# Layer 0's first MLP pair with seven block products for w4, and block sums of the weights added in DRAM

## The chip, the cores and the metric

The kernel runs on one core of a Trainium2 chip. The metric is device time in microseconds, lower is better. TensorE (PE) multiplies, VectorE (DVE) and ScalarE (ACT) do elementwise work, GpSimd (POOL) does small pieces of it, SyncE (SP) issues the DMAs. PEld is TensorE's loading of weights.

## The reference

Two layers, each an FNet mixing step and a shift MLP, on `x` of 2048 rows by 512 columns in float32:

```python
x = x + real(DFT_seq(DFT_hidden(layernorm(x))))         # dense DFT matrices
u = layernorm(x)
h = gelu(layernorm(u) @ w1)                             # 512 x 512
x1 = u + shift_quarters(h, +1, -1, +2, -2) @ w2         # 512 x 512
x = x + x1 + gelu(layernorm(x1) @ w3) @ w4              # 512 x 1376, 1376 x 512
```

## The kernel before

**Arithmetic.** Every float32 operand is kept as a rounded high part and a low part, the difference. A product is three matmuls (`mm3`, lines 294 to 296): high by high, high by low, low by high. ACT casts the high part, DVE subtracts for the low part. The weights of the matmuls lie 128 by 128 on the array; 512 or 256 columns stream past them.

**Fewer products.** Several matrix products are done by blocks with seven products in place of eight, after Strassen and Winograd: sums of blocks are made on both sides, and products are added up. On the weights' side of w3 a pair of 128-column tiles is cut in four blocks, and seven units per pair of tiles are kept: four block sums (units 0 to 3), three blocks as they are (4 to 6). The same holds for w4 in layer 1. In layer 0, w3 goes by seven products, w4 by eight.

**Order.** All work is in an order written out by hand (`manual_schedule`): each engine takes its instructions in the order of the program, so a step put at some place of the loop stands, on its engine, behind all that was put before it. One layer runs as follows.

- Layer 0's chunk 0 has a plain phase (`plain_phase`), in which the DFT's sequence product is made block by block. It calls `hook(0)` to `hook(15)`, one before each 24 matmuls.
- Each chunk c of 512 rows has an x phase (`x_phase`, for c > 0 in layer 0) and a y phase (`y_phase`). In the x phase eight steps k each call `hook(2k)` before 12 matmuls (banks C and B) and `hook(2k+1)` before 6 (bank A, with the DFT block's difference, an item "one"); ahead of `hook(2k)` stand 0, 12 or 24 matmuls of the hidden DFT of the chunk before (`HAT`). The y phase calls `hook(k)` before the first half of a step.
- DFT blocks come by DMA into four raw buffers (`raw`, line 222), are cast by ACT (lines 240, 243, 247) and completed by DVE (line 257) in a ring of four slots. `stream()` hands out the next slot and prepares the one three further.
- `by_pairs` then does the MLPs. First the spatial-shift part: 32 slots of 12 matmuls (`shifted`, `mixed`), with steps for DVE and ACT attached to slot numbers (`D(slot, ...)`, `A(slot, ...)`). Then two pairs of chunks go through w3, gelu and w4.

**The pairs.** In layer 0 both pairs run the loop over five pairs of tiles in `by_pairs`: seven w3 products (`prod`, 6 matmuls each), gelu, and w4 on the tiles before (`w4_part`, 12 matmuls of 512 columns for a tile and a chunk). In layer 1 the first pair is `first_pair`: w3 by seven products for all five pairs of tiles, the gelus kept, then 39 steps (`multiply`, 12 matmuls of 256 columns each) that take w4 by seven products; the second is `last_pair`.

**Weights.** The raw weights lie in `w34`. `w4_split(i)`, called from the plain phase's hooks i and from chunk 1's x phase as `w4_split(16 + i)`, takes 12 blocks of 128 by 512 (one of w3, 11 of w4) through four SBUF places `w4in`, one step per hook: block n is loaded by SP at hook n + 3, cast by ACT at n + 4, completed by DVE and stored by SP at n + 5 (to `w4d`, `w3e`). At one hook the store of block n − 2 comes first, then the cast of n − 1, then the load of n:

```python
for n in (i - 5, i - 4, i - 3):
    if n == i - 5:    # DVE low part; SP: dma_start(w4_from[n][1], w)
    elif n == i - 4:  # ACT: copy(w[:, 0], wf[:, 1])
    else:             # SP: dma_start(wf[:, 1], w4_from[n][0])
```

`w4_sums(k, i)` makes w4's block sums of one pair of tiles in SBUF, in five x phases of both layers (`W4_AT`), for layer 1's use. The units of w3 are made in layer 0's shift part (first pair of tiles) and in its first pair's loop (`w_prep`): SP loads `staged`, DVE makes four sums, ACT and DVE split them, SP keeps the result in `w3d`. Layer 0's second pair and layer 1 load `w3d`.

**Queues.** All DMAs are issued by SP, in the program's order; POOL issues none, and has only the small power and product steps of the layer norms (lines 313, 314, 334, 335).

Of the kernel before, what the change touches and what calls it, by code (L numbers as in the profile page):

```python
# [8 lines left out]
F32 = mybir.dt.float32  # L9
# [4 lines left out]
P = 128  # L14
# [29 lines left out]
def spectral_mlp_kernel(ctx: ExitStack, tc: tile.TileContext, x, ws, hs, w1, w2, w34, out):  # L44
# [7 lines left out]
    ident = const.tile([P, P], F32, name="ident")  # L52
    make_identity(nc, ident)
# [9 lines left out]
    w4s = [dram.tile([P, 4, 2, 2 * P], F32, name=f"w4s{i}") for i in range(NF // 2)]  # L63
    xtd = [dram.tile([D, CH], F32, name=f"xtd{i}") for i in range(2)]
# [52 lines left out]
    staged = at("staged", STG, 2, 2, 2 * P, dtype=F32)  # L117
# [19 lines left out]

    for i in range(WARM):
        nc.tensor.matmul(PD[1][:, :P], ident, ident, start=True, stop=True)  # L139
# [486 lines left out]
    def gelu(g, ps):  # L626
        order = "p (q b j) -> p b q j", "p (b q j) -> p b q j"
        g_of, ps_of = (v.rearrange(o, b=NB, q=TC) for v, o in zip((g, ps), order))
        nc.scalar.activation(g_of, ps_of, AF.Gelu_apprx_tanh)
# [79 lines left out]
    def b_sum(o, a, b):  # L709

        add(*(blkf[i][:, :, 1] for i in (o, a, b)), ALU.subtract)
# [12 lines left out]
    def by_pairs(layer, zs, xin, dst):  # L724
# [71 lines left out]
        order = [None] + fs + fs  # L796
        n_pairs = NC // 2
        seq, used = {"n": 0}, {"n": 0}

        def w4_slot(n):  # L800

            return n % 6 if n < len(order) else (n - len(order)) % 4

        def w4_load():
            n = seq["n"]
            if n == n_pairs * len(order) or n >= len(order) and n - used["n"] > 3:
                return
            src, i = order[n % len(order)], w4_slot(n)
            nc.sync.dma_start(w4r[i].bitcast(F32), w3e if src is None else w4d[src])
            seq["n"] += 1  # L810
# [4 lines left out]
        def w4_use():  # L815
            used["n"] += 1
            return w4r[w4_slot(used["n"] - 1)]

        def w3_load(n):
            if n >= n_pairs * (NF // 2):  # L820
                return
            if layer or n >= NF // 2:
                i = (n + (last_of(layer) and n >= NF // 2)) % 2
                nc.sync.dma_start(w3b[i].bitcast(F32), w3d[n % (NF // 2)])
                return
            nc.sync.dma_start(staged.rearrange("p f k w -> p f (k w)"), w34[2 * n : 2 * n + 2, :, 0].rearrange("f p w -> p f w"))

        def w3_sums(n, half):

            lo, (a, b) = w3bf[n % 2][:, 1], (staged[:, i] for i in range(2))  # L830
            if half == 0:
                add(lo[:, 2], a[:, 0], b[:, 0], ALU.subtract)
                add(lo[:, 0], b[:, 0], b[:, 1])
            else:
                add(lo[:, 1], lo[:, 0], a[:, 0], ALU.subtract)
                add(lo[:, 3], a[:, 1], lo[:, 1], ALU.subtract)

        def w3_of(n):
            return (slice(0, 4), w3bf[n % 2][:, 1, 0:4]), (slice(4, 6), staged[:, 0]), (slice(6, 7), staged[:, 1, 1:2])

        def w3_highs(n, *which):
            for i in which:
                units, src = w3_of(n)[i]
                nc.scalar.copy(w3b[n % 2][:, 0, units], src)

        def w3_lows(n, *which):
            w = w3b[n % 2]
            for i in which:
                units, src = w3_of(n)[i]
                nc.vector.tensor_tensor(w[:, 1, units], src, w[:, 0, units].bitcast(F32), op=ALU.subtract)  # L850

        def w3_keep(n):
            nc.sync.dma_start(w3d[n], w3b[n % 2].bitcast(F32))
# [63 lines left out]
        D(26, sum_of("t1", "12", "t1"))  # L917
# [10 lines left out]
        A(28, *([w3e_load] if last_of(layer) else [w4_load] * 4))  # L928
        if layer == 0:
            A(19, lambda: w3_load(0))  # L930
            D(23, lambda: w3_sums(0, 0))
            A(23, lambda: w3_highs(0, 1, 2))
            D(24, lambda: w3_sums(0, 1))
            A(24, lambda: w3_highs(0, 0))
            D(25, lambda: w3_lows(0, 0, 1, 2))
            A(25, lambda: w3_load(1))
            A(28, lambda: w3_keep(0))
        else:
            A(26, lambda: w3_load(0))
            A(28, lambda: w3_load(1))  # L940
            D(27, u_stats(2, 2))
            D(30, add_u(2, 0, 1, 2, 3))
# [16 lines left out]
        if not last_of(layer):  # L959
            w4_load()  # L960
            w4_load()
        gs = [tmp[:, 4], tmp[:, 5]]

        def w4_part(acc, f, h, beside=None):
            s = w4_use()
            for q in range(TC):
                if q == 2 and beside:
                    beside()
                v = slice(q * P, (q + 1) * P)
                mm3(acc[q], h[:, 0, v], h[:, 1, v], s[:, 0], s[:, 1], f == fs[0], f == fs[-1])  # L970
# [5 lines left out]
        bg, prep = [], {}  # L976

        def at_point(i):
            for f in prep.pop(i, ()):
                f()  # L980
# [60 lines left out]
        def z3_steps0(turned):  # L1041
            t = tmp[:, 0:4]
            return [
                lows("t3", "t4"),
                u_stats(2, 2),
                add_u(2, 0, 1, 2, 3),
                u_stats(3, 0),
                norm3(2, 0, 1),
                norm3(2, 2, 3),
                u_stats(3, 2),  # L1050
                lambda: (turn3(turned, 2, 0, 1)(), add_u(3, 0, 1)()),
                lambda: (turn3(turned, 2, 2, 3)(), turn_out(turned, z3d[2]), norm3(3, 0, 1)()),
                add_u(3, 2, 3),
                lambda: (norm3(3, 2, 3)(), turn3(t, 3, 0, 1)()),
                lambda: (turn3(t, 3, 2, 3)(), turn_out(t, z3d[3])),
            ]

        def next_block(c, half, to):
# [3 lines left out]
            4: [sum_of("t1", "12", "11")],  # L1062
# [9 lines left out]
        for pair in range(n_pairs):  # L1072
            c1, c2 = 2 * pair, 2 * pair + 1
            if last_of(layer):
                if pair == n_pairs - 1:
                    last_pair(c1, c2, dst, lambda: w4r[0])
                    continue
                loads = [next_block(*b) for b in ((3, 0, "12"), (2, 0, "11"), (2, 1, "21"), (3, 1, "22"))]
                first_pair(c1, c2, dst, z3_steps, loads, next_parts, w3_load, w3e_load)
                continue  # L1080
            kept, next_too = bool(layer or pair), pair == n_pairs - 1 and not last_of(layer)
            hcs = [hc[:, f] for f in range(NF)]
            if next_too:
                hcs[8:] = [hx[:, 0], hx[:, 1], rest[0]]
                bg += early
            if pair:
                bg.insert(0, lows("t4"))
            sets = [rest[4:8], rest[4:8]]
            bk, acc1 = (acc4, mm4) if pair == 0 else (mm4, acc4)
            acc2 = [bk[(1 + i) % 4] for i in range(4)]  # L1090
            if pair == 0:
                bg += z3_steps0(hc[:, 6:10])
            tmps[:] = gs
            s = w4_use()
            for i, names in enumerate((("11", "21"), ("12", "22"))):
                for d in range(KD):
                    b = blk[names[d // 2]]
                    v = slice(d * P, (d + 1) * P)
                    mm3(bk[i], s[:, 0, v], s[:, 1, v], b[:, d % 2, 0], b[:, d % 2, 1], d == 0, d == KD - 1)
                if i == 0:  # L1100
                    gelu_split(h4[2], bk[0], act)
                else:
                    gelu(hcs[NF - 1], bk[1])
                one()
            w4_load()

            def split_later(k):
                if k < NF:
                    split(h4[(2 + k) % 4], hcs[fs[k]], act)

            def next_blocks(*which):

                for c, half, to in which:
                    b_in(c, half, to)

            def w_prep(p):

                n = p + 1
                if n == NF // 2:
                    return {}  # L1120
                return {
                    0: [lambda: w3_sums(n, 0), lambda: w3_highs(n, 1, 2)],
                    1: [lambda: w3_sums(n, 1), lambda: w3_highs(n, 0)],
                    2: [lambda: w3_lows(n, 1, 2), *[lambda: w3_load(n + 1)] * (n + 1 < NF // 2)],
                    4: [lambda: w3_lows(n, 0), lambda: w3_keep(n)],
                }

            for p in range(NF // 2):
                prep = {} if kept else w_prep(p)
                u, v, x, y = sets[p % 2]  # L1130
                w = w3b[(5 * pair + p) % 2]
# [7 lines left out]
                if pair:  # L1139
                    one()  # L1140
# [791 lines left out]
```

## Time and profile before

| | |
|---|---|
| median of 3 runs | 1420.42 us (1420.28 to 1420.55) |
| profiled execution | 1420.21 us |
| its span, first to last instruction | 1418.3 us |
| TensorE clock granted | 1.0 throughout |
| bytes moved | 306.31 MB, 216 GB/s |

The profile is one execution. Its page gives each engine's busy time, the span in 40 slices with busy tenths, the DMA queues, the chain of work that ended last, and the costliest groups. Answers to narrower questions give a stretch's busy times, or single instructions with start and duration in us and, in brackets, how long their engine was idle before and what released it. "ACT w4in L1662: 10.5, 9" under "who waited for it" reads: these instructions' tiles kept line 1662 on ACT waiting 10.5 us in all, at 9 places. A queue named SPq is SP's issue of DMAs; "to landing" is from issue to the data being there.

### The profile page before, as it was taken

To read this page: it belongs to the slowest core of one execution; us is meant where nothing else is said; L and a number is where in the kernel's file an instruction comes from. 1 tells how busy PE (TensorE), PEld (TensorE's weight loads), DVE (VectorE), ACT (ScalarE), POOL (GpSimd) and SP (SyncE) were. 2 spreads that over 40 slices of the span, in tenths; PEclk is the share of its full clock that TensorE was granted. 3 is DMA by queue.
4 is the path that set the end of the run, shared out by engine and by line. 5 is a ranking of instruction groups with operands and counts; after the bars stand their busy time and mean duration, and the time that the engine had idled before them with its cause. 6 is when DMAs were issued, how large, how long until landed. Compare 5 with 4: busy or idle time off the path is not lost.

```text
span 1418.3 us, 17864 instructions
## 1 busy us (share of the span) xinstructions
PE 1413.0 (100%) x6465; PEld 1177.7 (83%) x6465; DVE 1186.4 (84%) x1675; ACT 740.8 (52%) x1007; POOL 77.9 (5%) x105
## 2 busy tenths in 40 slices
PE   9999999999999999999999999999999999999998
PEld 8888888888888888888888888888888888899887
DVE  7986998988979888666789989989889788897676
ACT  6663464455566754434555544644555656454351
POOL 2100000000001000000000000000000020000000
PEclk9999999999999999999999999999999999999999
DMA  7867647658753857945556476575597457677864
GB/s 256 278 208 237 208 153 262 194 164 308 240 164 98 292 205 261 357 159 187 193 176 214 149 262 200 172 262 169 194 309 238 134 141 245 189 247 240 311 207 158
DMA packets 136488, 306.31 MB, mean 216 GB/s; under 512 B 9680, under 2 KB 58064, under 8 KB 133712
## 3 DMA queue, kind: packets, MB, share of 16 engines
q1 hardware_dynamic: 136400, 305.17, 64.6%
q8 instruction: 51, 0.84, 0.2%
q14 instruction: 37, 0.30, 0.1%
HBM read 250.87 MB, written 54.26 MB: 215 GB/s over the span
## 4 chain that ended last, share of the span: by engine, by line
PE 94%; DVE 3%; ACT 1%; issue 1%; POOL 0%; DVEq 0%; POOLq 0%; ACTq 0%
PE psd L294 10%; PE psd L295 10%; PE psd L296 9%; PE psa L295 8%; PE psa L294 8%; PE psa L296 8%; PE psc L295 7%; PE psb L295 7%; PE psb L294 7%; PE psb L296 7%; PE psc L296 7%; PE psc L294 7%; DVE rest L480 0%; ACT tmp L342 0%; PE psd L139 0%
## 5 line engine op out<-in xcount | busy, mean ns | idle before, releaser
L240 ACT CAST ring<-raw 128x1024 fp32r<-128x1024 f32 x127 | 133.1, 1052 | 79.3 <-PE psd L296 43.2
L257 DVE TENSOR_TENSOR ring<-raw,ring 128x1024 fp32r<-128x1024 f32 x126 | 153.4, 1219 | 13.1 <-ACT ring L240 12.9
L294 PE MATMUL psd<-ring,rr 128*128 128x512 f32 x208 | 80.9, 389 | 0.0
L295 PE MATMUL psd<-ring,rr 128*128 128x512 f32 x208 | 80.9, 389 | 0.0
L296 PE MATMUL psd<-ring,rr 128*128 128x512 f32 x208 | 80.9, 389 | 0.0
L334 POOL TENSOR_TENSOR rs<-ve,mhalf 128x4 f32<-128x4 f32 x16 | 27.0, 1685 | 723.9 <-DVE nm L333 723.9
L247 ACT CAST ring<-ring0f 128x1024 fp32r<-128x1024 f32 x28 | 29.5, 1054 | 50.7 <-DVE ring0f L246 50.7
L257 DVE TENSOR_TENSOR ring<-ring1f,ring 128x512 fp32r<-128x512 f32 (+1 forms) x56 | 53.2, 950 | 0.7 <-ACT ring L243 0.7
L313 POOL TENSOR_TENSOR rs<-ve,mhalf 128x2 f32<-128x2 f32 (+2 forms) x33 | 28.8, 873 | 415.1 <-DVE nb L312 405.6
L342 ACT ACTIVATE tmp<-xs,nb,rs 128x512 f32<-128x512 f32 x56 | 43.3, 810 | 15.6 <-POOL nb L314 14.4
L294 PE MATMUL psc<-ring,ay 128*128 128x512 f32 x128 | 49.8, 389 | 0.0
L295 PE MATMUL psc<-ring,ay 128*128 128x512 f32 x128 | 49.8, 389 | 0.0
L296 PE MATMUL psc<-ring,ay 128*128 128x512 f32 x128 | 49.8, 389 | 0.0
L294 PE MATMUL psb<-ring,ay 128*128 128x512 f32 x128 | 49.8, 389 | 0.0
L295 PE MATMUL psb<-ring,ay 128*128 128x512 f32 x128 | 49.8, 389 | 0.0
L296 PE MATMUL psb<-ring,ay 128*128 128x512 f32 x128 | 49.8, 389 | 0.0
L295 PE MATMUL psa<-ring,ay 128*128 128x512 f32 x126 | 49.0, 389 | 0.0
L296 PE MATMUL psa<-ring,ay 128*128 128x512 f32 x126 | 49.0, 389 | 0.0
L294 PE MATMUL psa<-ring,ay 128*128 128x512 f32 x126 | 49.0, 389 | 0.0
L294 PE MATMUL psd<-ring,ay 128*128 128x512 f32 x126 | 49.0, 389 | 0.0
L295 PE MATMUL psd<-ring,ay 128*128 128x512 f32 x126 | 49.0, 389 | 0.0
L296 PE MATMUL psd<-ring,ay 128*128 128x512 f32 x126 | 49.0, 389 | 0.0
(826 smaller groups left out, 4488.7 us busy)
## 6 DMA issues: line engine op xcount, KB each, us to landing
raw<-in_ws SPq DMA_DIRECT2D x183, 512.0 KB, 5.1
raw<-in_hs SPq DMA_DIRECT2D x56, 512.0 KB, 3.6
w4r<-w4d SPq DMA_DIRECT2D x44, 512.0 KB, 4.6
w3b<-w3d SPq DMA_DIRECT2D x10, 1792.0 KB, 9.0
w3d<-w3b SPq DMA_DIRECT2D x5, 1792.0 KB, 6.8
x1d<-tmp SPq DMA_DIRECT2D x12, 512.0 KB, 6.2
xs<-x1d SPq DMA_DIRECT2D x12, 512.0 KB, 5.0
w4d<-w4in SPq DMA_DIRECT2D x11, 512.0 KB, 4.8
```

The source lines that it names most:

```text
L240: nc.scalar.copy(dest[:, a:b, 0], r[0][:, a:b])
L247: nc.scalar.copy(dest[:, :, 0], lo)
L257: nc.vector.tensor_tensor(lo, src, hi.bitcast(F32), op=ALU.subtract)
L294: nc.tensor.matmul(o, lh, rh, start=first, stop=False, skip_group_check=more)
L295: nc.tensor.matmul(o, lh, rl, start=False, stop=False, skip_group_check=more)
L296: nc.tensor.matmul(o, ll, rh, start=False, stop=last, skip_group_check=more)
L313: nc.gpsimd.tensor_tensor(rs[:, :n], ve[:, :n], mhalf[:, 0, :n], op=ALU.pow)
L334: nc.gpsimd.tensor_tensor(rs, ve, mhalf[:, :, :2], op=ALU.pow)
L342: nc.scalar.activation(o, s, AF.Identity, bias=mr[2], scale=mr[1])
```

## The change

- Layer 0's first pair now runs `first_pair`, as layer 1's does; the loop in `by_pairs` is left with layer 0's second pair, and w4 tiles come through four SBUF places, not six.
- All units of w3 and w4 are made ahead of the pair. `w4_split` becomes `w_split` with 20 entries: behind the 12 of before stand five of w3's blocks 4 and 5 and three loads with the blocks 6 of two pairs of tiles (the last has one). The appended ones run on into chunk 1's x phase.
- The block sums are made in DRAM tensors `sum3` and `sum4`. Step 0 of `sums_of` is five copies by SP (one per pair of tiles) of one block into four places; steps 1 to 3 are five DMAs each, issued by POOL, that add a block onto places 0 to 2, 1 to 3 and 2. w3's steps stand at hooks 0, 4, 8 and 12 of chunk 1's x phase, w4's at those of chunk 2's.
- The sums are loaded, split and kept at hooks of chunks 1 to 3 (`sum_at`) and, for two sums of w4, in the shift part.
- Signs change so that all weight sums are additions; units are in another order; some sums of activations and gelus take the sign. `first_pair` runs one of the last steps earlier. Chunk 2's statistics and residual sums move into the shift part in layer 0, too.
- The identity for the first matmuls lies in the arena. POOL's DMA scratch is 1024 bytes for 512.

```diff
-    w4_from = [(w34[NF - 1][:, 0], w3e)] + [(w34[f + LAG][:, 1], w4d[f]) for f in range(NF)]
-    def w4_split(i):
...
-    def w4_sums(k, i):
...
+    halves3 = [w34[2 * i : 2 * i + 2, :, 0].rearrange("f p (h w) -> f h p w", h=2) for i in range(NF // 2)]
+    halves4 = [w34[2 * i + LAG : 2 * i + LAG + 2, :, 1].rearrange("f p (h w) -> h f p w", h=2) for i in range(NF // 2)]
+    split_from = [(w34[NF - 1][:, 0], [w3e])] + [(w34[f + LAG][:, 1], [w4d[f]]) for f in range(NF)]
+    split_from += [(w34[2 * i][:, 0], [w3d[i][:, :, 4:6].rearrange("p r u w -> p r (u w)")]) for i in range(NF // 2)]
+    for i in range(0, NF // 2, 2):
+        src = w34[2 * i + 1 : min(2 * i + 5, NF - 1) : 2, :, 0, 2 * P :].rearrange("f p w -> p f w")
+        split_from.append((src, [w3d[k][:, :, 6] for k in range(i, min(i + 2, NF // 2))]))
+    def w_split(i):
+        for n in (i - 5, i - 4, i - 3):
...
+    def sums_of(to, blocks, i):
+        (r, c), (a, b) = (((1, 0), (0, 4)), ((0, 0), (0, 3)), ((1, 1), (1, 4)), ((0, 1), (2, 3)))[i]
+        for k in range(NF // 2):
+            src = blocks[k][r, c].unsqueeze(1).broadcast_to([P, b - a, 2 * P])
+            if i:
+                nc.gpsimd.dma_start(to[k][:, a:b], src, accum_op=ALU.add)
+            else:
+                nc.sync.dma_start(to[k][:, a:b], src)
...
+    for i in range(4):
+        prepare[1, "x", 4 * i] = [lambda i=i: sums_of(sum3, halves3, i)]
+        prepare[2, "x", 4 * i] = [lambda i=i: sums_of(sum4, halves4, i)]
+    sum_at(1, "y", sum_a, 3, 0, 3, 5, 6)
+    sum_at(2, "x", sum_a, 3, 1, 0, 4, 5)
+    sum_at(2, "x", sum_b, 3, 3, 1, 5, 6)
+    sum_at(2, "x", sum_a, 3, 2, 7, 11, 12)
+    sum_at(2, "y", sum_a, 3, 4, 1, 3, 4)
+    sum_at(3, "x", sum_a, 4, 0, 1, 5, 6)
+    sum_at(3, "x", sum_b, 4, 2, 2, 6, 7)
+    sum_at(3, "x", sum_a, 4, 1, 8, 12, 13)
...
@@ x phase, layer 0: hook(i)
-                    w4_split(2 * NP + i)
+                    w_split(2 * NP + i)
-                if (layer, c) in W4_AT:
-                    w4_sums(W4_AT[layer, c], i)
+                if layer == 0:
+                    prepare_at(c, "x", i)
...
@@ by_pairs
+        first_pair(0, 1, dst, z3_steps, loads, next_parts, w3_load, w3e_load if last_of(layer) else w4_load)
-        nc = bacc.Bacc("TRN2", target_bir_lowering=False, num_devices=1, dynamic_dma_scratch_size=512)
+        nc = bacc.Bacc("TRN2", target_bir_lowering=False, num_devices=1, dynamic_dma_scratch_size=1024)
```

The four numbers behind `sum_at`'s places and kind are the pair of tiles and the hooks of the load, the cast and the low part with the stores.

More of the change, by code (lines that the diff above doesn't have):

```diff
@@ L816, in w4_use @@
             used["n"] += 1
-            return w4r[w4_slot(used["n"] - 1)]
+            return w4r[(used["n"] - 1) % 4]
         def w3_load(n):
[L820 to L853, printed above, removed]
+            if n < n_pairs * (NF // 2):
+                nc.sync.dma_start(w3b[(n + (n >= NF // 2)) % 2].bitcast(F32), w3d[n % (NF // 2)])
         sc0, sc1, sc2 = scratch
@@ L1417, in first_pair @@
                 drain(n - 2)
-        for n, c in ((-2, c1), (-1, c2)):
-            drain(len(steps) + n)
-            for j in range(c * TC, c * TC + TC, 2):
-                rows(xs[j // 2], dst, j, 2, False)
+        drain(len(steps) - 1)
+        for j in (*range(c2 * TC, c2 * TC + TC, 2), *range(c1 * TC, c1 * TC + TC, 2)):
+            rows(xs[j // 2], dst, j, 2, False)
         w3_load(nk + 1)
```

482 lines of the change are left out of this document (215 added, 267 removed).

## The prediction

> **What bounds the kernel now.** I read the page's first, second and fourth parts, then stretches of the run one by one.
>
> ```profile
> span 1418.3 us, 17864 instructions
> PE 1413.0 (100%) x6465; PEld 1177.7 (83%) x6465; DVE 1186.4 (84%) x1675; ACT 740.8 (52%) x1007; POOL 77.9 (5%) x105
> DMA  7867647658753857945556476575597457677864
> PE 94%; DVE 3%; ACT 1%; issue 1%; POOL 0%; DVEq 0%; POOLq 0%; ACTq 0%
> ```
>
> TensorE is busy from end to end and is 94% of the chain that ended last, so a matmul taken away is time won, and what another engine loses counts only where TensorE then waits. DMA engines are busy about two thirds of the time, and that will matter.
>
> The next rows are stretches: layer 0's plain phase; chunk 1's x and y phase and chunk 2's x phase, where the change puts its new transfers; the spatial-shift part; layer 0's first MLP pair; layer 1's first pair. Behind the length stand the busy times of PE, PEld, DVE, ACT and POOL, the clock, the DMA share and GB/s.
>
> ```profile
> 8.00:95.00 87.00, 87.00 (x383) 71.81 (x384) 73.39 (x132) 56.43 (x81) 11.96 (x16) 1.00 0.76 255
> 95.00:150.00 55.00, 55.00 (x244) 45.53 (x244) 42.69 (x54) 27.95 (x35) 2.83 (x2) 1.00 0.66 220
> 150.00:194.00 44.00, 44.00 (x196) 36.44 (x195) 41.38 (x46) 21.81 (x26) 2.23 (x2) 1.00 0.53 168
> 194.00:248.00 54.00, 54.00 (x240) 44.72 (x239) 46.79 (x57) 27.75 (x33) 2.83 (x2) 1.00 0.71 242
> 411.00:496.00 85.00, 85.00 (x376) 70.29 (x375) 69.47 (x136) 58.10 (x92) 11.21 (x16) 1.00 0.60 188
> 496.10:609.00 112.90, 112.90 (x499) 93.47 (x498) 88.88 (x144) 51.75 (x78) 3.02 (x6) 1.00 0.75 272
> 1201.20:1308.00 106.80, 106.75 (x704) 96.81 (x704) 91.68 (x143) 51.14 (x81) 1.79 (x4) 1.00 0.67 210
> ```
>
> **Part 1: the matmuls of layer 0's first pair.** Start, duration, instruction: the first matmul of each first pair and of the pair after it, then two neighbours of 512 and two of 256 columns.
>
> ```profile
> 496.13 0.39 PE L294 MATMUL psc<-b,w4r 128*128 128x512 f32 x1
> 609.01 0.39 PE L294 MATMUL psd<-b,w4r 128*128 128x512 f32 x1
> 1201.24 0.39 PE L294 MATMUL psc<-b,w4r 128*128 128x512 f32 x1
> 1307.99 0.39 PE L294 MATMUL psd<-b,w4r 128*128 128x512 f32 x1
> 515.17 0.39 PE L294 MATMUL psb<-bt,w3b 128*128 128x512 f32 x1
> 515.39 0.39 PE L295 MATMUL psb<-bt,w3b 128*128 128x512 f32 x1
> 1264.81 0.28 PE L294 MATMUL psd<-un,hr 128*128 128x256 f32 x1
> 1264.93 0.28 PE L295 MATMUL psd<-un,hr 128*128 128x256 f32 x1
> ```
>
> What a matmul costs is the distance to its neighbour, not its own 0.39. Layer 0's first pair has 24 + 210 + 264 = 498 matmuls of 512 columns (edge, w3, w4) in 609.01 − 496.13 = 112.88 us, 0.2267 each. The change gives it the code of layer 1's first pair: 24 + 210 of those, and for w4 39 steps of 12 matmuls with 256 columns (half, 0.113) in place of 264 with 512. By count that is 264 × 0.2267 − 468 × 0.1133 = 59.8 − 53.0 = 6.8 us less; layer 1's pair really takes 1307.99 − 1201.24 = 106.75, 6.1 less. I take **−6.1**, since the same code will have the same short waits; the ends are −6.8 and 0 (if its units or parts come late).
>
> **Part 2: the longer chain of weight splits.** Before, 12 blocks pass through `w4_split`, one per hook: DMA in at hook n+3, ACT's copy at n+4, DVE's low part and DMA out at n+5. All but the last low part lie in the plain phase, where a hook comes every 24 matmuls, 5.4 us. The change appends eight blocks (12 to 19), and their copies fall on hooks 0 to 7 of chunk 1's x phase, where 6 to 36 matmuls lie between hooks, 1.4 to 8.2 us. ACT works in order, so a copy that waits for its load holds the cast of the next DFT block, and TensorE waits for that.
>
> ```profile
> DMA to landing us min/median/max: 3.4/5.2/7.7
>   ACT w4in L1662: 10.5, 9
> 85.66 0.38 SPq L1664 DMA_DIRECT2D w4in3f<-in_w  x1
> 92.27 0.33 SPq L1660 DMA_DIRECT2D w4d<-w4in  x1
> 97.00 0.33 SPq L1660 DMA_DIRECT2D w4d<-w4in  x1
> 98.39 0.68 DVE L378 TENSOR_TENSOR ay7f<-tmp 128x512 f32<-128x512 f32 x1
> L1662 ACT CAST w4in<-w4in3f x3: 621/621/622, 49.8 to 90.9; 128x512 fp32r<-128x512 f32 x3
> L1659 DVE TENSOR_TENSOR w4in<-w4in3f,w4in x3: 680/684/685, 52.0 to 96.3; 128x512 fp32r<-128x512 f32 x3
> 101.19 0.62 ACT L243 CAST ring<-ring2f 128x512 fp32r<-128x512 f32 x1
> 107.06 0.39 PE L294 MATMUL psa<-ring,ax 128*128 128x512 f32 x1
> 114.11 1.05 ACT L240 CAST ring<-raw 128x1024 fp32r<-128x1024 f32 x1 [1.67 <-PE psd L296]
> 117.56 0.62 ACT L243 CAST ring<-ring1f 128x512 fp32r<-128x512 f32 x1 [2.40 <-DVE ring1f L242]
> 118.19 1.05 ACT L240 CAST ring<-raw 128x1024 fp32r<-128x1024 f32 x1
> 123.38 0.39 PE L294 MATMUL psa<-ring,ax 128*128 128x512 f32 x1
> ```
>
> The first two rows are the line of the split loads: 3.4 to 7.7 us to landing, and even at the plain phase's pace ACT waited 10.5 us for them in nine of twelve copies. Load n is issued behind the store of n−2, which needs the low part of n−2, which needs copy n−2. So copy n comes at least 5.2 (landing) + 0.62 (copy) + 0.68 (low) + 0.33 + 0.38 (issues) = 7.2 us behind copy n−2. Load 12 goes out behind the store at 92.27 and lands about 97.9; load 13 behind the one at 97.00 lands about 102.6. Left alone, copies 14, 16, 18 come at 105.1, 112.3, 119.5 and 15, 17, 19 at 109.8, 117.0, 124.2. Copy 19 stands ahead of the cast at 118.19, which then begins at 124.8: some 2 us of TensorE's time already.
>
> **Part 3: the burst.** In the same hook 0, right behind load 13, SP issues five DRAM-to-DRAM copies of 512 KB, 2.62 MB.
>
> ```profile
> raw<-in_ws SPq DMA_DIRECT2D x183, 512.0 KB, 5.1
> w3b<-w3d SPq DMA_DIRECT2D x10, 1792.0 KB, 9.0
> u<-w4s SPq DMA_DIRECT2D x10, 512.0 KB, 8.9
> 100.24 0.33 SPq L222 DMA_DIRECT2D raw<-in_ws  x1
> 107.26 1.06 ACT L240 CAST ring<-raw 128x1024 fp32r<-128x1024 f32 x1 [0.67 <-PE psb L296]
> 113.86 0.39 PE L294 MATMUL psc<-ring,ax 128*128 128x512 f32 x1
> 124.45 1.98 POOL L334 TENSOR_TENSOR rs<-ve,mhalf 128x4 f32<-128x4 f32 x1 [55.63 <-DVE nm L333]
> ```
>
> 1280 KB more took 9.0 − 5.1 = 3.9 us: 336 GB/s. No row shows a copy inside DRAM; at that rate the burst is 7.8 us of all engines (ends: 0, if it runs beside the rest; 7.8). Load 14 is issued at about 100.5 (DVE is busy to 99.07, then 0.68, 0.33 and 0.38), 2.7 us into the burst, and lands 5.2 + 7.8 − 2.7 = 10.3 later, at 110.8. Copy 14 stands ahead of the cast at 101.19; that item is then ready at 110.8 + 0.62 + 0.62 + 0.68 = 112.7 (copy, cast, low), while TensorE wanted it at 107.06: a stall of 5.6.
>
> **Part 4: the adding transfers.** POOL issues 15 of them in this phase (5 × 896 KB, 4.59 MB), 15 in chunk 2's. POOL is idle from 68.8 to the row at 124.45 (55.63 before it), so they wait for nothing but the burst's landing and run from about 108 on, while links 16 and 18 are loaded; L334 queues behind them, but its results are first read past 411. No row has an adding transfer. The nearest for a crowded queue is the 512 KB that took 8.9 in layer 1's last pair against 5.1 commonly, 3.8 more; I add that to each of the two links (ends: 0; 5.2, a doubled landing). Copy 18 is then at 110.8 + 2 × 11.0 = 132.8, ahead of the cast at 117.56; that item is ready at 134.7 and was wanted at 123.38. The phase's stall is **+11.3**, the 5.6 within it. From below it is 0 (all landings at 3.4, burst beside them); from above it is engine time: 0.66 × 55 = 36.3, plus eight splits of 0.79 MB 18.7, burst 7.8, adding 13.7, makes 76.5 us in 55, **21.5** over.
>
> A rule of the Trainium skill bears on the +3.8: by "DMA: Bandwidth & Descriptors", section "Queues, rings and completion order", an engine takes turns, packet by packet, between the queues with work for it. Taken at its word, SP's loads run at half rate while POOL's add; the two links would be 5.2 longer each, and the sum 2.8 higher than mine, 1430.2. In the run before only one queue moves data, so no row tests it.
>
> **Part 5: chunk 2's x phase** has a burst and adding too, but no splits. The shortest lead of a DFT load in the rows is 107.26 − 100.24 = 7.0; 1.9 are spare after a landing of 5.1. Behind a burst it is 5.4 later, with crowding 9.2; 7.3 late at the cast. That cast's item is used at 113.86, so 113.86 − 107.26 − 1.06 less a low part of some 1.4 (twice the 0.68 of half its width) = 4.1 are covered, and 3.2 remain. Between 0 and 3.2 I take **+2.0**, since crowding holds only while POOL adds. The ends are 0 and 15.1: engine time 0.71 × 54 + 7.8 + 13.7 + 14.0 (three sums of 0.52 MB loaded and 1.05 kept) − 4.7 (the w4 sums gone) = 69.1 in 54.
>
> **At nothing:** the w3 preparation leaves the first pair and the spatial-shift part, where DVE had room (88.88 of 112.90, 69.47 of 85.00). Chunk 2's statistics and sums move into the shift part, six DVE instructions of 0.68, 4.1 us, into 15.5 of idle (4.1 if those were gone); so do two w4 sums, 3.1 MB or 9.4 us of engine time in the 0.40 × 85 free. Block sums of w4 leave five x phases: DVE and ACT are relieved, TensorE did not wait for them. Split lows add 8 × 0.68 to DVE's 42.69 of 55 (5.4 without its idle). Four w4 slots for six in the second pair, `ident` in the arena, the signs: the same instructions.
>
> **The sum:** −6.1 + 11.3 + 2.0 = +7.2 on the profiled execution's 1420.21, **1427.4** (it lies 0.21 under the median of 1420.42). 0.2%, 2.8 us, is about what a measurement of this kernel tells from no change.
>
> **Rivals.**
> 1. *Covered (faster).* Split loads land in 3.4 to 4.5, the burst passes beside them, so no copy holds ACT over what the ring covers. For it: landings of 3.4 occur, TensorE was never idle in these phases, DVE has 12 us free. Against: ACT waited at a slower pace. It decides as long as both phases' stalls stay under 3.3. With 1.5 of them the time is 1420.2 − 6.1 + 1.5 = 1415.6.
> 2. *Burst alone (same).* Adding is slow and thin, only the 5.6 stand: 1419.7. For it: DMA's idle third. Against: POOL's free start.
> 3. *DMA the bound in both phases:* 21.5 + 15.1 − 6.1, 1450.7. For it: the engine sums. Against: 20 us of free engine time in each y phase.
> 4. *The saving doesn't come,* units or parts late in the first pair: 1420.2 and more. Against: layer 1's same code ran in 106.75.
>
> **Numbers.** Forecast 0.40 (own range 1423 to 1440), rival 1 0.35, rival 2 0.19, rival 3 0.03, rival 4 0.03. Faster 0.35, same 0.21, slower 0.44. From 1413 (all of 6.8, some noise) to 1435, about 0.15 is left out, nearly all above.
>
> **What would show it.** Right: the first pair near 106.8; between 100 and 135 TensorE idle with releaser ring lows, ACT idle on `w4in` loads, their landings of 8 us and more. Wrong: TensorE unbroken there, ACT's waits on `w4in` under 15 us, span some 6 less: then landings or the burst were mispriced.

## The result, and the profile after

The kernel with the change takes 1471.67 us (median; 1469.67 to 1472.49) against 1420.49 us (1420.28 to 1420.66): a ratio of 1.0358 [1.034, 1.0376]. The profiled execution took 1471.52 us. The forecast was 1427.4 with a range up to 1435: slower was right, the size was not.

From the page of the kernel after, in the order of the page: span, TensorE's busy time, the clock and DMA slices, the chain that ended last.

```profile
span 1469.6 us, 18517 instructions
PE 1423.9 (97%) x6669; PEld 1188.2 (81%) x6669; DVE 1192.5 (81%) x1674; ACT 744.3 (51%) x1024; POOL 107.1 (7%) x135
PEclk9997998999999999999999999999999999999999
DMA  7879988998974585776375557476487537587864
PE 76%; DVE 8%; DMA 7%; issue 6%; ACT 2%; POOL 1%; SPq 1%; DVEq 0%; ACTq 0%; POOLq 0%
```

TensorE was 100% busy and 94% of the chain; now it is idle for 46 us, and a quarter of the chain belongs to others. The slices (36.7 us each) place it: the DMA engines are 80% busy or more in slices 4 to 9, and the clock dips in slices 4 and 7. By stretches, after, with the columns of the prediction's table (length, busy PE, PEld, DVE, ACT, POOL, clock, DMA share, GB/s): chunk 1's x and y phase, chunk 2's x phase, chunk 3's x phase, the shift part, layer 0's first pair.

```profile
93.64:173.42 79.78, 63.03 (x247) 49.10 (x246) 47.65 (x63) 31.51 (x45) 10.58 (x9) 0.87 0.97 284
173.42:225.39 51.97, 44.26 (x187) 35.86 (x186) 39.75 (x43) 20.04 (x23) 9.16 (x10) 0.93 0.83 218
225.39:292.82 67.43, 59.29 (x247) 47.87 (x246) 50.22 (x59) 30.96 (x40) 7.77 (x8) 0.92 0.98 296
...
334.98:393.17 58.19, 56.35 (x247) 46.02 (x246) 48.51 (x57) 30.61 (x39) 9.74 (x9) 1.00 0.92 302
457.09:550.55 93.46, 89.98 (x385) 72.92 (x384) 71.41 (x141) 59.16 (x94) 12.36 (x18) 0.98 0.66 210
550.55:657.30 106.75, 106.68 (x703) 96.78 (x702) 91.42 (x143) 50.31 (x81) 1.78 (x4) 1.00 0.68 220
```

Measured from each stage's first matmul to the next one's, the same stages took 55.76, 42.16, 55.76, 55.76, 87.15 and 112.88 us before. So the differences are +24.0, +9.8, +11.7, +2.4, +6.3 and -6.1; chunk 2's y phase, chunk 3's y phase and the hidden part have none, the second pair and layer 1 have +0.9 each, and 1.4 lie outside these stages: 51.3 us, the difference of the spans.

**Chunk 1's x phase**, single instructions of SP, ACT and TensorE:

```profile
98.03 5.20 SPq L1581 DMA_DIRECT2D sum<-in_w  x5
103.33 3.90 SPq L1565 DMA_DIRECT2D w3d<-w4in  x1
107.27 0.91 SPq L1570 DMA_DIRECT2D w4in2f<-in_w  x1
119.00 0.62 ACT L1567 CAST w4in<-w4in2f 128x512 fp32r<-128x512 f32 x1 [12.53 <-DMA w4in2f<-in_w]
119.53 0.61 ACT L243 CAST ring<-ring2f 128x512 fp32r<-128x512 f32 x1
120.19 0.80 PE L294 MATMUL psa<-ring,ax 128*128 128x512 f32 x1 [11.57 <-ACT ring L243]
...
126.13 0.63 PE L294 MATMUL psd<-ring,rr 128*128 128x512 f32 x1
126.56 0.63 PE L295 MATMUL psd<-ring,rr 128*128 128x512 f32 x1
```

The issue of the five copies alone holds SP for 5.20 us and that of the store behind them for 3.90, where a DFT load's issue took 0.33 before. Load 14 goes out at 107.27, lands 11.7 us later, ACT stands 12.53 us before its copy, and the cast behind it is what TensorE waits for. The last two rows are 0.43 us apart, not 0.227: TensorE runs at half rate for some microseconds after such a wait.

**Chunk 1's y phase**: the group of adding transfers on the page (busy, mean ns, idle before), POOL's first three and one of the late ones, SP's instructions, its waits at the line of the sum loads (ns: shortest, median, longest), and TensorE's wait from the list of waits.

```profile
L1579 POOL DMA_DIRECT2D sum<-in_w x30 | 33.6, 1178 | 238.5 <-issue 145.2
```

```profile
107.44 1.47 POOL L1579 DMA_DIRECT2D sum<-in_w  x1 [38.45 <-DMA sum<-in_w]
120.01 1.24 POOL L1579 DMA_DIRECT2D sum<-in_w  x1 [11.10 <-DMA w4in3f<-in_w]
128.83 1.23 POOL L1579 DMA_DIRECT2D sum<-in_w  x1 [7.58 <-issue]
...
198.94 1.24 POOL L1579 DMA_DIRECT2D sum<-in_w  x1 [8.06 <-issue]
```

```profile
184.43 7.09 SPq L222 DMA_DIRECT2D raw<-in_ws  x4
208.51 0.59 SPq L1588 DMA_DIRECT2D sumaf<-sum  x1
```

```profile
L1588 SPq EVENT_SEMAPHORE  x15: 17/28/16905, 191.6 to 506.0; - x15
```

```profile
PE psb L294 <- ACT ring L247: 7.2, 1, 7.2
```

POOL issues one add about every 10 us, and the last of the fifteen of w3 goes out after 210. SP reaches the load of the first sum at 191.6, stands 16.9 us at its semaphore until the last add onto this sum (issued at 205.33) is done, and issues no DFT load in that time. ACT then waits for the sum's landing too, and TensorE waits 7.2 us for the casts behind it.

**Chunk 2's x phase**: the second burst, the sum loads behind it, and the DFT load behind those.

```profile
229.14 5.76 SPq L1581 DMA_DIRECT2D sum<-in_w  x5
235.07 2.17 SPq L1588 DMA_DIRECT2D sumaf<-sum  x1
...
240.58 1.17 SPq L222 DMA_DIRECT2D raw<-in_ws  x1
252.64 0.79 PE L294 MATMUL psc<-ring,ax 128*128 128x512 f32 x1 [6.67 <-ACT ring L240]
```

### The profile page after: what moved, and what is told of

The parts are those of the page before. It is cut to its first block, busy times and chain, and to the rows that moved or that the text cites. A ratio compares the mean times of both kernels' runs of the same rounds, so it can differ in the third digit from the quotient of the medians.

```text
span 1469.6 us, 18517 instructions
## 1 busy us (share of the span) xinstructions
PE 1423.9 (97%) x6669; PEld 1188.2 (81%) x6669; DVE 1192.5 (81%) x1674; ACT 744.3 (51%) x1024; POOL 107.1 (7%) x135
## 3 DMA queue, kind: packets, MB, share of 16 engines
q0 software_dynamic: 9440, 9.18, 4.4%
## 4 chain that ended last, share of the span: by engine, by line
PE 76%; DVE 8%; DMA 7%; issue 6%; ACT 2%; POOL 1%; SPq 1%; DVEq 0%; ACTq 0%; POOLq 0%
PE psd L296 7%; PE psd L294 7%; PE psd L295 7%; PE psa L294 6%; PE psa L296 6%; PE psa L295 6%; PE psb L295 6%; PE psb L296 6%; PE psb L294 6%; PE psc L295 6%; PE psc L294 5%; PE psc L296 5%; DMA z3d<-scr 1%; DVE ring L257 1%; DMA w4in2f<-in_w 1%
## 5 line engine op out<-in xcount | busy, mean ns | idle before, releaser
L294 PE MATMUL psd<-ring,rr 128*128 128x512 f32 x208 | 82.6, 397 | 2.4 <-ACT ring L240 2.4
L295 PE MATMUL psd<-ring,rr 128*128 128x512 f32 x208 | 82.7, 398 | 1.2 <-DVE ring L257 1.2
L296 PE MATMUL psd<-ring,rr 128*128 128x512 f32 x208 | 82.1, 395 | 0.0
L294 PE MATMUL psa<-ring,ax 128*128 128x512 f32 x112 | 44.3, 396 | 11.6 <-ACT ring L243 11.6
L257 DVE TENSOR_TENSOR ring<-ring2f,ring 128x1024 fp32r<-128x1024 f32 (+1 forms) x40 | 42.5, 1061 | 14.9 <-ACT ring L247 11.4
L1579 POOL DMA_DIRECT2D sum<-in_w x30 | 33.6, 1178 | 238.5 <-issue 145.2
L294 PE MATMUL psc<-ring,ax 128*128 128x512 f32 x112 | 44.2, 395 | 6.7 <-ACT ring L240 6.7
L342 ACT ACTIVATE tmp<-xs,nb,rs 128x512 f32<-128x512 f32 x56 | 43.3, 810 | 13.7 <-POOL nb L314 13.7
L294 PEld LDWEIGHTS psd<-ring,rr 128*128 128x128 f32 x208 | 39.9, 192 | 11.9 <-ACT ring L240 3.5
L294 PE MATMUL psa<-ring,ay 128*128 128x512 f32 x126 | 49.2, 390 | 0.0
```

The source lines that it names most:

```text
L257: nc.vector.tensor_tensor(lo, src, hi.bitcast(F32), op=ALU.subtract)
L294: nc.tensor.matmul(o, lh, rh, start=first, stop=False, skip_group_check=more)
L295: nc.tensor.matmul(o, lh, rl, start=False, stop=False, skip_group_check=more)
L296: nc.tensor.matmul(o, ll, rh, start=False, stop=last, skip_group_check=more)
L342: nc.scalar.activation(o, s, AF.Identity, bias=mr[2], scale=mr[1])
L1579: nc.gpsimd.dma_start(to[k][:, a:b], src, accum_op=ALU.add)
```

## The experiments

Each run is told by its losses against the kernel before, stage by stage, worked out from the first matmuls of the stages as above; the other stages are within 1.3 us (adds_only also loses 4.9 at the end of its plain phase). The losses are those of one profiled execution each. The times of after and of best1 to best6 are medians of four or five, the others single executions; for best3 the profiled one took 1429.2, for the other five within 1 us of the median. The kernel before, measured beside them, took 1420.4 to 1420.7.

| us | time | 1 x | 1 y | 2 x | 3 x | 3 y, hidden | shift | first pair |
|---|---|---|---|---|---|---|---|---|
| after | 1471.7 | 24.0 | 9.8 | 11.7 | 2.4 | 0.0 | 6.3 | -6.1 |
| no_adds | 1444.6 | 17.3 | 0.0 | 5.8 | 0.7 | 0.0 | 5.3 | -6.1 |
| plain_adds | 1458.0 | 24.0 | 0.0 | 8.8 | 0.7 | 0.0 | 8.2 | -6.1 |
| no_split | 1462.3 | 10.0 | 16.9 | 9.7 | 2.7 | 1.3 | 5.9 | -6.1 |
| no_sums | 1433.6 | 10.3 | 0.0 | 0.5 | 2.5 | 0.0 | 5.8 | -6.1 |
| spread_alone | 1426.8 | 1.2 | 0.0 | 0.5 | 2.4 | 0.0 | 7.8 | -6.1 |
| burst_only | 1435.4 | 7.9 | 0.0 | 5.6 | 0.7 | 1.3 | 5.6 | -6.1 |
| adds_only | 1446.4 | 3.4 | 10.6 | 2.7 | 2.0 | 1.1 | 6.5 | -6.1 |
| free_loads | 1462.1 | 26.7 | 0.0 | 10.8 | 3.1 | 0.0 | 5.4 | -6.1 |
| ring2048 | 1474.6 | 32.6 | 0.0 | 18.6 | 0.8 | 0.0 | 6.2 | -6.1 |
| best1 | 1438.6 | 0.2 | 0.0 | 9.0 | 7.1 | 5.6 | 0.8 | -6.1 |
| best3 | 1427.2 | 4.2 | 0.0 | 2.4 | 3.9 | 1.4 | 2.1 | -6.1 |
| best4 | 1431.9 | 1.6 | 0.0 | 9.4 | 3.6 | 0.8 | 1.4 | -6.1 |
| best5 | 1430.1 | 0.4 | 0.0 | 6.3 | 6.9 | 0.4 | 0.9 | -6.1 |
| best6 | 1427.6 | 0.3 | 0.0 | 5.1 | 2.4 | 0.4 | 3.1 | -6.1 |

**no_adds.** 

> Left out: the 30 adding transfers on POOL (steps 1 to 3 of sums_of), so the block sums are the first block alone; burst, split chain and loads of the sums stay. Theory A (slow adding: the adds run one at a time, some 10 us each, so the sums are late, and SP's queue stands behind the load of a sum): chunk 1's y phase falls from +9.8 to under +1, chunk 2's x phase from +11.7 to about +5 (its burst), chunk 1's x phase from +24.0 to about +12; 1440 to 1448. Theory B (DMA engine time: the engines are full from 98 to 335 us and adds are dear packets): the same direction, and the DMA share of 104 to 170 falls below 0.9. Theory C (burst and split chain alone make chunk 1's x phase late): that phase stays at +20 or more; 1450 to 1460.

```diff
-            if i:
-                nc.gpsimd.dma_start(to[k][:, a:b], src, accum_op=ALU.add)
-            else:
+            if not i:
                 nc.sync.dma_start(to[k][:, a:b], src)
```

```profile
104.00:170.00 66.00, 54.52 (x216) 42.32 (x215) 43.75 (x56) 29.14 (x40) 1.43 (x2) 0.90 0.85 282
```

1444.6. The y phase is whole again and chunk 2's x phase loses 5.8, as A forecast; but B's sign, a DMA share under 0.9, came too (0.85), so this run does not tell A from B. Chunk 1's x phase still loses 17.3, between A's 12 and C's 20: burst and chain are most of it. By the difference, the adds cost it 6.7.

**plain_adds.** 

> Changed: POOL's 30 transfers copy and do not add (the sums are wrong). Bytes, rows, queue and order stay. Theory A, its cause the queue (POOL's scratch holds the descriptors of one such transfer at a time): still one issue every 9 to 11 us, and the time stays within 6 us of 1471.7. Theory B (an adding packet is what is dear, 110 ns for 1 KB): an issue every 4 to 6 us, y phase of chunk 1 back to under +2, 1440 to 1455.

```diff
-                nc.gpsimd.dma_start(to[k][:, a:b], src, accum_op=ALU.add)
+                nc.gpsimd.dma_start(to[k][:, a:b], src)
```

1458.0, between the two. From the part on queues, POOL's queue after and here:

```profile
q0 software_dynamic: 9440, 9.18, 4.4%
```

```profile
q0 software_dynamic: 2720, 9.18, 1.8%
```

```profile
107.18 0.94 POOL L1579 DMA_DIRECT2D sum<-in_w  x1 [37.62 <-DMA sum<-in_w]
108.56 0.74 POOL L1579 DMA_DIRECT2D sum<-in_w  x1 [0.44 <-DMA sum<-in_w]
116.71 0.74 POOL L1579 DMA_DIRECT2D sum<-in_w  x1 [7.41 <-issue]
```

The same bytes go in 2720 packets for 9440, and for 1.8% of the engines' time for 4.4%. Two transfers follow each other within 1.4 us, and the fifteen are out in 66 us, not 103. So adding is the dearer form, as B said, and there is a limit to how many are under way, as A said. Chunk 1's x phase did not gain: plain copies in the adds' place cost it as much.

**no_split.** 

> Left out: the eight appended splits (units 4 to 6 of the w3 tiles get one block unsplit, copied inside DRAM at five hooks of chunk 3's y phase). Burst, adds and sums stay. Theory C (ACT's in-order copies of the split chain hold the casts): chunk 1's x phase falls from +24.0 to +8 or less, 1453 to 1458. Against it (the burst and the adds alone crowd the loads of the DFT blocks): that phase stays at +16 or more, 1463 to 1470.

```diff
-    split_from += [(w34[2 * i][:, 0], [w3d[i][:, :, 4:6]...]) for i in range(NF // 2)]
-    for i in range(0, NF // 2, 2):
-        ...
@@ chunk 3's y phase, hook(k), k < 5
+                    for r in range(2):
+                        nc.sync.dma_start(w3d[k][:, r, 4:7], halves3[k][0, 0].unsqueeze(1).broadcast_to([P, 3, 2 * P]))
```

1462.3. The x phase falls from 24.0 to 10.0, nearer to theory C, but the y phase loses 16.9 for 9.8: TensorE gets there sooner, the adds do not, and SP stands longer at the sum's load. Part of what a stage gains is lost at the next one's wait.

**no_sums** and **spread_alone.** 

> Left out: burst and adds; the loads of the sums stay at their hooks with their bytes, but read blocks of the weights and wait for no sum. What is left is the longer split chain, the loads, casts, low parts and stores of ten sums, and the first pair with fewer matmuls. My prediction's term for the chain alone: chunk 1's x phase +2, the first pair -6.1, so about 1416 to 1419. If the matmuls run at half rate behind each idle stretch, or loads and stores of the sums cost: +4 to +8, 1420 to 1426. If the shift part still loses its 6.3 us, the sums' own loads do that.

> Left out, as in no_sums: burst and adds. Changed against it: the eight appended splits no longer come one per hook at hooks 0 to 7 of chunk 1's x phase, but with a load every second hook, ACT's copy three hooks behind its load, up to hook 3 of the y phase. The same loads, copies, low parts and stores are done. Theory C1 (what costs the 10.3 us is copies that stand ahead of casts before their loads have landed): the x phase falls from +10.3 to under +3, no half-rate stretch, 1423 to 1427. Theory C2 (the 6.3 MB of split traffic fill the DMA engines, share 0.86, wherever in the phase they stand): still +6 or more there, 1429 to 1434.

```diff
 no_sums
-        prepare[1, "x", 4 * i] = [lambda i=i: sums_of(sum3, halves3, i)]
-        prepare[2, "x", 4 * i] = [lambda i=i: sums_of(sum4, halves4, i)]
-            nc.sync.dma_start(f[:, :, 1], src[:, v])
+            nc.sync.dma_start(f[:, :, 1], src[0, 0].unsqueeze(1).broadcast_to([P, v.stop - v.start, 2 * P]))
 spread_alone, besides: place and hooks of load, copy, low part of the eight (16 and more: y phase)
+    later = ((0, 0, 3, 4), (1, 2, 5, 6), (2, 4, 7, 8), (0, 6, 9, 10), (1, 8, 11, 12), (0, 12, 15, 16), (1, 14, 16, 17), (0, 16, 18, 19))
```

Chunk 1's x phase with the chain alone, crowded, then spread:

```profile
93.85:159.88 66.03, 60.62 (x248) 47.70 (x246) 48.21 (x64) 31.95 (x44) 1.44 (x2) 0.95 0.82 272
```

```profile
93.70:150.70 57.00, 56.09 (x248) 46.07 (x247) 45.84 (x60) 30.72 (x41) 1.70 (x2) 1.00 0.81 280
```

The chain alone costs 10.3 us, where the prediction had 2. With the same loads, copies and stores at other hooks it costs 1.2, at the same DMA share (0.82, 0.81). (In spread_alone the first sum's steps stand one hook later, too.) So not the bytes cost but the copies that stand in ACT's order ahead of casts, theory C1. Both runs still lose 5.8 and 7.8 in the shift part, with no sum to wait for: the sums' own loads and stores do most of that (versions below without a sum there lose 0.8 to 1.4). Its rows in no_sums:

```profile
466.92 3.66 SPq L614 DMA_DIRECT2D zd<-scr  x4
470.62 0.69 SPq L1588 DMA_DIRECT2D sumb0f<-in_w  x1
473.89 0.37 SPq L619 DMA_DIRECT2D zt1f<-zd  x1
...
482.17 1.05 ACT L438 CAST zt<-zt1f 128x1024 fp32r<-128x1024 f32 x1 [2.62 <-DMA zt1f<-zd]
```

The w4 sum's load stands between the transposed block's store and its reload; the reload lands 8.3 us after its issue, ACT waits for it, and TensorE is idle for 2.1 us up to 489.6 behind a block's low part.

**burst_only** (the edits of no_split and no_adds together) and **adds_only.** 

> Left out: the appended splits (filled in as in no_split) and the adds; the bursts, and the loads of the sums, stay. The phase with split chain alone lost 10.3 us, with burst and chain 17.3, with all three 24.0, with burst and adds 10.0. If the parts add up, the burst costs 4 to 7 alone in chunk 1's x phase and 5 in chunk 2's; if burst and chain cost only through each other, under 2 in chunk 1's. 1426 to 1436.

> Left out: the appended splits (filled in as in no_split). Moved: the five copies of each burst, one per hook, into the plain phase (for w3) and chunk 1's y phase (for w4), so that the adding transfers stand alone in the two x phases. If the parts add up, chunk 1's x phase loses the 2.1 us by which burst and adds (10.0) stand over the burst (7.9), chunk 1's y phase 8 to 17 as long as its sum's load stands in SP's queue before the adds are done, and chunk 2's x phase 2 to 5; 1432 to 1445. If an add is slow because the queues are crowded, its landing falls from 9.0 to 5 us or less and the y phase loses under 3; 1422 to 1428. If it is slow by itself, the landing stays at 8 to 10 us.

```diff
 adds_only, on no_split
-    for i in range(4):
+    for i in range(1, 4):
         prepare[1, "x", 4 * i] = [lambda i=i: sums_of(sum3, halves3, i)]
...
+    for k in range(NF // 2):
+        prepare[0, "p", 2 * k + 3] = [lambda k=k: sums_of(sum3, halves3, 0, k)]
+        prepare[1, "y", k] = [lambda k=k: sums_of(sum4, halves4, 0, k)]
```

The burst alone costs 7.9 and 5.6 us in the two x phases. The adds alone, in adds_only, in chunk 1's x phase, in two stretches:

```profile
98.40:104.00 5.60, 5.60 (x13) 4.44 (x14) 5.60 (x10) 3.08 (x8) 1.23 (x1) 0.50 0.85 169
104.00:157.50 53.50, 53.48 (x234) 43.83 (x234) 37.89 (x47) 25.76 (x31) 7.78 (x6) 0.99 0.82 238
```

The phase's 3.4 us are half rate in its first 5.6 us (clock 0.50), behind an idle 4.6 us at the end of the plain phase, where the moved copies stand. After it TensorE does not stop once, with four adds in the stretch: adds beside an otherwise undisturbed phase cost nothing there. Beside the burst they cost 2.1 (10.0 for 7.9), beside burst and chain 6.7. They still take 9.2 us (median) to land, so an add is slow without burst and splits, too, and the y phase loses 10.6 at the sum's load.

**free_loads.** 

> Changed: the loads of the sums read blocks of the weights (same hooks, bytes and places), so that they wait for no adding transfer; burst, adds and split chain stay (the sums go unused). If chunk 1's y phase loses its 9.8 us because SP's queue stands behind the load of a sum that is not yet added: that phase is back under +1, chunk 2's x phase keeps its burst and crowding (+6 to +12); 1459 to 1464. If the crowding by the adds itself starves the loads of the DFT blocks: the y phase still loses 5 or more, 1467 to 1473.

```diff
-            nc.sync.dma_start(f[:, :, 1], src[:, v])
+            nc.sync.dma_start(f[:, :, 1], src[0, 0].unsqueeze(1).broadcast_to([P, v.stop - v.start, 2 * P]))
```

The y phase, without its start:

```profile
176.40:218.40 42.00, 42.00 (x187) 34.74 (x186) 41.06 (x44) 21.98 (x26) 9.52 (x9) 1.00 1.01 264
```

No idle time with w3's adds still under way and a DMA share of 1.01: the 9.8 us were SP's order, not crowding.

**ring2048.** 

> Changed: POOL's DMA scratch is 2048 bytes for 1024 (room made by packing some small tiles of the statistics together); all else as after, nothing left out. If the scratch holds the descriptors of one adding transfer at a time and the next waits for it to drain: pairs of adds go out close together, 15 of them in 50 to 70 us for 103, and chunk 1's y phase falls from +9.8 to under +2; 1455 to 1464. If an add is slow by itself (its 1 KB packets read and write DRAM), the pace stays near 10 us and the time within 4 of 1471.7.

```diff
-dynamic_dma_scratch_size=1024
+dynamic_dma_scratch_size=2048
```

```profile
107.80 2.74 POOL L1578 DMA_DIRECT2D sum<-in_w  x2 [38.59 <-DMA sum<-in_w]
120.59 1.24 POOL L1578 DMA_DIRECT2D sum<-in_w  x1 [10.04 <-issue]
```

Two adds now go out together, so the scratch does hold them back. (In the run after, each of the first ten adds goes out as the one before it has landed: those issued at 107.44, 120.01 and 128.83 landed 12.3, 8.5 and 10.4 us later, and the next came at 120.01, 128.83 and 139.50.) Fifteen take 84 us for 103, the sums are done in time, and the y phase loses nothing, but chunk 1's x phase loses 32.6 for 24.0 and chunk 2's 18.6 for 11.7. The total does not move (1474.6): the loss went from one stage to two others.

**Versions for all of it.** 

> A version for all of it, nothing left out: the block sums are made in SBUF by four additions on POOL from the raw blocks (no burst, no adding transfers; load and store of a sum as before), the appended splits are spread over chunk 1's x and y phase, and the two w4 sums leave the spatial-shift part (one goes into chunk 3's y phase, one into the hidden part behind it). If the theories hold (the split chain's place, burst, adds and the sums in the shift part are what costs, and the first pair keeps its -6.1): losses of 0 to 3 us in all, 1414.5 to 1418. If the moved statistics alone cost the shift part its 5 us: 1419 to 1422. If POOL's additions are late for ACT's casts: a phase with +3 or more, 1422 to 1430.

> Another version for all of it, nothing left out. Against best1 the four additions of a sum are on DVE, not on POOL (there they took 1.4 to 2.5 us each, ACT's casts waited for them, and DVE's 128x1024 operations beside them took 1.75 us for 1.22); every sum has at least three hooks between load and additions; one sum each stands in chunk 1's x phase, chunk 2's y phase, the hidden part and early in the shift part, three each in chunks 2 and 3's x phases. If POOL was what cost best1 its 21 us in chunk 2 and 3: each phase within 1 us of before, 1414.5 to 1417.5. If the DMA engines are too full for three sums in an x phase, or DVE has no room for additions and low parts (2.7 us per sum): +2 to +4 in those phases, 1418 to 1425.

> best3 with other places, nothing left out. There the loads of residual rows (hook 10 of an x phase) stood behind 1 MB of stored sums, and ACT's casts of sums stood in the same hook as DVE's additions. Now the stores fall on hooks 5 to 8 or on 15, a cast stands one hook behind its additions, chunk 3's x phase has two sums for three, and the shift part none; chunk 1's and chunk 3's y phases take one each. If placing is all that was left: phases within 1 us of before, shift part +0.8 (the moved statistics), 1415.5 to 1419.5, faster than before. If DVE's y phases (41 of 44 us busy) have no room for 2.7 us more: +1 to +3 in each, 1419 to 1425.

> Nothing left out. Against best4: splits placed as in best1 (chunk 1's x phase lost 0.2 there), no sum in that phase; in chunks 2 and 3's x phases three sums each with casts at hooks 6, 8 and 12 (best4's late third sum at hooks 13 to 15 had TensorE wait at the start of the y phase, best3's first at hook 4 at its start). If placing is what cost best3 and best4: x phases of chunks 2 and 3 lose under 2 each, all losses together 3 to 6, 1417.5 to 1420.5. If three sums are too much for an x phase wherever they stand: +3 and more in each, 1421 to 1428.

> Nothing left out. best5 with two sums in chunk 3's x phase and the third early in the shift part (hooks 3 to 9). If three sums are too much for an x phase: chunk 3's falls from best5's loss to under 1, for 1 more in the shift part. If placing alone counts: the same as best5 within 1 us, 1417.5 to 1421.5.

```diff
-                nc.gpsimd.dma_start(to[k][:, a:b], src, accum_op=ALU.add)
+    def sum_add(places, kind):
+        for o, x, y in ((0, b(1, 0), b(0, 0)), (3, b(1, 0), b(1, 1)), (1, to(0), b(1, 1)), (2, to(1), b(0, 1))):
+            nc.gpsimd.tensor_tensor(to(o), x, y, op=ALU.add)     # best1; from best3 on: DVE
```

Ratios: best1 1.0122 [1.0105, 1.0139], best3 1.0044 [1.0027, 1.006], best4 1.0086 [1.0073, 1.01], best5 1.0066 [1.0049, 1.0082], best6 1.0052 [1.0037, 1.0067]. All keep the pair's -6.1 and take most of the 51 us back; none beats the kernel before, and all five took longer than forecast. In best1 TensorE waits for DVE's low parts, and DVE is slowed by POOL's additions (last section); how much of its loss that is stays open, since best4 loses 9.4 in chunk 2's x phase without them. Something of what is left in the others, by SP and DVE in best6, chunk 2's x phase:

```profile
228.65 2.54 SPq L1617 DMA_DIRECT2D w3d<-sumb  x4
231.24 1.31 SPq L204 DMA_DIRECT2D x1d<-tmp  x1
...
238.52 0.38 SPq L204 DMA_DIRECT2D tmp<-in_x  x1
...
243.00 1.29 DVE L479 TENSOR_TENSOR tmp<-psd,tmp 128x512 f32<-128x512 f32 x2 [5.54 <-DMA tmp<-in_x]
```

The residual rows are stored from and loaded into the same place (hooks 9 and 10). Behind the stores of a sum the store of the rows is late, their load with it, and DVE, in order, stands 5.5 us before them with the low parts of the ring behind it. best6 against best5 (three sums or two in chunk 3's x phase) gave 4.5 us there and lost 2.2 in the shift part, so the number in a phase counts. Chunk 2's x phase is the same code in both and differs by 1.2, so smaller differences between these versions say nothing. A schedule that keeps the whole saving was not found, and whether there is one stays open.

## Why the prediction was wrong, point by point

- **Part 1, the pair: right.** 106.75 us, -6.1, in every run with the change.

```profile
550.56 0.39 PE L294 MATMUL psc<-b,w4r 128*128 128x512 f32 x1
657.31 0.39 PE L294 MATMUL psd<-b,w4r 128*128 128x512 f32 x1
```

- **Part 2, the chain: mechanism right, size wrong.** "Some 2 us" alone was 10.3. Its copies 16 to 19 came at 115.1, 119.1, 124.5 and 129.9 in no_sums, for 112.3, 117.0, 119.5 and 124.2 forecast: links of 8.4 to 10.8 us for 7.2. Not the landings made them long (5.1 to 5.5 for 5.2, one of 7.1), but what lies between a copy and the next load but one: 2.2 to 5.2 us for my 2.0, because the low part stands in DVE's order and the load in SP's. After copy 17, at 119.11, the low part began at 122.38. Half rate, which the sum does not have, is 2.6 of the 10.3. And I asked only of the last copy whether it was late.
- **Part 3, the burst: this step failed first.** I gave its five issues no time and had load 14 go out at 100.5; SP needed 5.20 + 3.90 us for the issues and it went at 107.27. Its landing, 11.7, was near the 10.3 forecast. The idle stretch was 11.6 us for 5.6. Why these issues take so long no run shows.
- **Part 4, the adding transfers: the term was near, its meaning was not.** +5.7 for the x phase, 6.7 by no_adds. Split loads 16 to 19 landed 1 to 3 us later with adds than without (8.0 for 5.0, 6.0 for 5.0, 8.9 for 7.3, 6.5 for 4.7), for my 3.8, so that the sum came near is partly luck. The 5.2 that I worked out from the rule of the Trainium skill's "DMA: Bandwidth & Descriptors", "Queues, rings and completion order", turns by packet between queues, came out too dear. What failed: I priced fifteen adds at 13.7 us of engine time (they took 103) and asked who waits for POOL, but not who waits for the sums. SP does, in order, and that is the y phase's 9.8, a term that the sum does not have.
- **Part 5, chunk 2's x phase: +2.0 was 11.7.** The same two steps: 5.76 us to issue the burst, 5.2 for the sum loads behind it, and adds to the end of the phase. (That a load behind the burst is 5.4 later has no working there; Part 3 has 5.1.)
- **"At nothing": the shift part lost 6.3.** The w4 sums there were counted as engine time, with room for it; they stand in SP's queue between a block's store and its reload. Where no sum stood there, in best1, best5 and best4, 0.8, 0.9 and 1.4 remain: the moved statistics cost about 1. Chunk 3's 2.4 were not priced either, and their cause stays open. DVE's and ACT's relief was worth nothing, as forecast.
- **Rivals.** The third came nearest (1450.7), with engine sums of 76.5 us for the x phase that lasted 79.8 at a share of 0.97. But it is not shown right: spread_alone and free_loads have TensorE busy beside the chain or the adds, at 0.81 and 1.01. The share tells that transfers are under way, not that one is late; what was late stood behind something in an order. No run has burst and adds beside the spread chain, so whether the engines would bound the x phase with all three in it stays open. The fourth rival, units late in the pair, did not occur.
- **Signs.** Those named came: landings of 11.7, 11.6 and 8.0 us, ACT idle for 12.53 us on a `w4in` load, and TensorE idle behind it, though released there by a cast and not by a low part.
- The range was too narrow because the ends of each part were bounded by engine time and never by the time of a queue that waits.

## What to carry to other kernels

Follow each new transfer in both directions: how long its issue holds the queue it is issued from, and what stands in that queue behind the instruction that waits for its result. A transfer in DRAM that looks free by its bytes can cost its reader's whole queue. When work is put beside a full engine, spread it and give each load several steps before the in-order engine that consumes it; a copy that is asked for one step after its load turns every slow landing into a stall.

## What the runs showed of the hardware that I had not expected

- **Half rate after idle time.** Matmuls of 512 columns are 0.427 us apart for some 2 to 6 us after TensorE was idle (clock 0.50 in the first adds_only row above). By neighbours between 0.40 and 0.45 us apart it cost 3.2 us in chunk 1's x phase after, and about 7.5 us in all. Taken by TensorE's idle time, as in the brackets above, no single stretch of up to 1.6 us brought it in any run; of those from 1.7 to 2.3 us some did, and of the longer ones most. The Trainium skill, "TensorE: Matmul & The Clock Gate", Part 1, puts it at an idle window of about 3.4 us; the measurement has it after shorter idle stretches.
- **An add is slow.** 384 KB took 9.2 us (median) to land in adds_only, without bursts in the x phases and without the appended splits; plain copies of the same bytes took 7.7 in plain_adds, two at a time. In DRAM the adding form moves 1 KB per packet (9440 packets for 9.18 MB), the plain one 3.4 KB. Whether the packets or the adding make it slow no run tells.
- **POOL's additions slow DVE's.** The same DVE operation in best1, with POOL idle and with POOL adding, and POOL's additions:

```profile
200.13 1.22 DVE L479 TENSOR_TENSOR rr01f<-rr01f,tmp 128x1024 f32<-128x1024 f32 x1
...
212.60 1.75 DVE L479 TENSOR_TENSOR rr00f<-rr00f,tmp 128x1024 f32<-128x1024 f32 x1
...
211.56 6.21 POOL L1594 TENSOR_TENSOR sumaf<-sumaf 128x256 f32<-128x256 f32 x4
```

1.22 us become 1.75, and the four additions of 256 columns take 6.2 us. The Trainium skill, "SBUF — State Buffer", section "SBUF: two separate sides", says that a DVE operation with two SBUF inputs and a GpSimd one that reads SBUF lock each other out; the trace agrees. On DVE the same four take 1.6 us (best6):

```profile
232.97 1.55 DVE L479 TENSOR_TENSOR sumaf<-sumaf 128x256 f32<-128x256 f32 x4
```
